# A fixed start order, a route in three steps, and a gate that ScalarE sums, in an attention and two-MoE kernel

## The chip, the cores and the metric

The kernel runs on one core of one Trainium2 chip. The metric is the device time of one execution in microseconds, as the median of several runs. TensorE is PE, VectorE DVE, ScalarE ACT, GpSimd POOL and SyncE SP.

## The reference

```python
# x: 8 batches, 8 heads, 576 tokens, 64 columns a head; 4608 tokens of 512 in all
kv = einsum('bhsd,bhde', q, einsum('bhsd,bhse->bhde', k, v))   # linear attention, no softmax
x = kv / sqrt(mean(kv*kv, -1) + 1e-6) * g_norm
# MoE1, dense: d_model 512, d_ff 1536
g = x @ w_gate;  x = (g * sigmoid(g) * (x @ w_val)) @ w_out
# MoE2: 8 experts, d_ff 1024; a token with x @ w_skip <= 0 is passed through
logits = xc @ w_gate2;  e = argmax(logits)
p = exp(logits - max(logits));  p /= sum(p) + 1e-9
y = p[e] * (relu(xc @ w1[e]) @ w2[e]);  out = xc + y
```

All is float32.

## The kernel before

The 4608 tokens go in 12 chunks of 384 (three rows of 128). A matmul in float32 is made of parts: each operand is split into a high and a low part (the ScalarE copy makes the high one, line 254 on POOL or VectorE the low one), and three products are summed.

**Attention.** Two heads are a pair, four pairs `pr` a chunk. `attn_load` loads k and v of a pair (`kv`, as 112 and 4 partitions, by `spread`) and its q (`qt`). `attn_unit` makes `kvp` (L211), copies it into `kvbd` (L213, L214), multiplies (`op`, L227), squares on ScalarE (`sq`, L233), reduces on VectorE (`ms`, L235 and L236), takes the power on POOL (`y`, L238) and scales (`xn`, L240). `make_xT` transposes that (`xtps`, L262) into `xT` (L265, L266). The units of chunk c+1 are worked between the steps of chunk c; those of chunk 0 stand at the program's start.

**MoE1.** A chunk takes 12 steps f. A step has 24 matmuls `gv` (L346), the silu (L352), a product on VectorE (`s`, L353), its split `hT` (L355, L254) and 9 matmuls `acc` (L367). The 18 weight tiles come in another number format and are converted during chunk 0: six VectorE instructions of about 0.7 us each tile (`split_bits`, L286, L287 and L290), with ScalarE (L284, L296) and POOL. They stay in the 18 buffers of pool `wp`; before that, four of these hold the q of chunk 0.

**Route.** The logits of chunk c−1 are worked on VectorE in chunk c, as 27 instructions `dump` (L400), 3 a step and 4 in the last chunk. Then `chunk_route` finds the expert and the place of each row (L432 to L452), with two small matmuls `rp` (L446, L447), and POOL scatters the rows to memory (`xs`, L454). The last chunk's own logits are made on TensorE: transposes `ltp` (L411) and matmuls `lps` (L416).

**MoE2.** Batches of up to 384 rows of one expert: batch 0 the first 256 rows of the fullest expert, ranked on the rows up to the chunk before the last, batch 1 the rest of it, then one batch for each other expert, and a rest. `load_xe` loads a batch's rows (L601, on `n // nt` partitions), `make_gate` makes the softmax weight (L584 to L591: maximum, difference, exponential, sum, reciprocal) and `make_xT2` transposes (`xtp`, L618; `xU`, L621 and L623). A step f has 12 matmuls `hp` (L633), the relu and split `h2T` (L641, L642), and matmuls `yacc` (L721) or `tacc` (L687). Expert weights `v` are split by ScalarE (L567) and by POOL or VectorE (L254). Work of batch 0 is interleaved with the end of the last chunk.

Each engine runs its instructions in order. That order isn't written by hand: the framework's scheduler takes the instructions in program order with a model of time and sets the order on each engine, within the dependencies and the orderings that `after(ins, to)` adds. SP issues nearly all loads, in order; a load whose completion lane or buffer is not free holds up those behind it.

Of the kernel before, what the change touches and what calls it, by code (L numbers as in the profile page):

```python
# [29 lines left out]
def attention_moe_moe_kernel(  # L30
# [97 lines left out]

    def attn_qt_load(c, pr):
        if c == 0:  # L130

# [4 lines left out]
        if c % 3 == 1:
            cut = S - T
            nc.gpsimd.memset(t[:, cut:cut + P], 0.0)
            nc.sync.dma_start(t[:, 0:cut], src[:, 0:cut])
            nc.sync.dma_start(t[:, cut + P:], src[:, cut:])  # L140
        else:
            nc.sync.dma_start(t[:, 0:T], src)
        qt[c, pr] = t

    def attn_load(c, pr):
        if c % 3 != 2:
            b = 2 * (c // 3) + c % 3
            t = p2.tile([P, 2, NR, P], F32, tag="kv", name="kv")
            for lo, hi in spread(PK):
                nc.sync.dma_start(t[lo:hi], kv_d[b, pr, lo:hi])  # L150
            kvt[c, pr] = t
        attn_qt_load(c, pr)

    attn_load(0, 0)


# [248 lines left out]
    def logits_pe(c, w9):  # L405
        lp = ps_acc.tile([P, R, P], F32, tag="acc", name="lps")
        for r in range(R):
            st = xrow[c, r]
            tp = ps_x.tile([P, NK, P], F32, tag="px", name="ltp")
            for kk in range(NK):  # L410
                nc.tensor.transpose(tp[:, kk, :], st[:, kk * P:(kk + 1) * P], ident)  # L411
# [3 lines left out]
            for kk in range(NK):  # L415
                nc.tensor.matmul(  # L416
# [7 lines left out]
    def chunk_route(c):  # L424
        lg = lgt.pop(c)
        wd = wdesc.rearrange("p (o e) -> p o e", o=1).to_broadcast([P, R, E])
        eb = (elast if c == NCH - 1 else ebase).rearrange("p (o e) -> p o e", o=1).to_broadcast([P, R, E])
# [19 lines left out]
        nc.tensor.matmul(rp, onesb, ca[:, 0:R, :], start=False, stop=True)  # L447
        nc.vector.tensor_tensor(oh, rp, eb, op=ALU.add)
# [128 lines left out]
    def make_gate(x, n, tag, q=P):  # L577
# [442 lines left out]
```

## Time and profile before

| | us |
|---|---|
| median of 3 runs | 1309.68 (1309.29 to 1310.69) |
| the profiled execution | 1305.69 |
| its span, first to last instruction | 1304.0 |
| PE busy | 1266.1 (97%) |
| POOL busy | 510.6 (39%) |
| DVE busy | 639.3 (49%) |
| ACT busy | 373.5 (29%) |

The mean granted clock of TensorE is 0.995 of full. A share of busy time is an average over the whole span; DVE at 49% is nine tenths busy in chunk 0 and a third in the last stage.

### The profile page before, as it was taken

To read this page: it belongs to the slowest core of one execution; us is meant where nothing else is said; L and a number is where in the kernel's file an instruction comes from. 1 tells how busy PE (TensorE), PEld (TensorE's weight loads), DVE (VectorE), ACT (ScalarE), POOL (GpSimd) and SP (SyncE) were. 2 spreads that over 40 slices of the span, in tenths; PEclk is the share of its full clock that TensorE was granted. 3 is DMA by queue.
4 is the path that set the end of the run, shared out by engine and by line. 5 is a ranking of instruction groups with operands and counts; after the bars stand their busy time and mean duration, and the time that the engine had idled before them with its cause. 6 is when DMAs were issued, how large, how long until landed. Compare 5 with 4: busy or idle time off the path is not lost.

```text
span 1304.0 us, 18975 instructions
## 1 busy us (share of the span) xinstructions
PE 1266.1 (97%) x7239; PEld 1180.2 (91%) x7239; DVE 639.3 (49%) x1487; ACT 373.5 (29%) x773; POOL 510.6 (39%) x545
## 2 busy tenths in 40 slices
PE   5998999999999999999999999999999989999997
PEld 5987999999999999999999999999988978899996
DVE  5896817237164371542815418146283243544662
ACT  3664112122121221211212112121122433344441
POOL 4674323233322332223323223223346443566662
PEclk9999999999999999999999999999999999999999
DMA  9663702021120111202102021110121343555631
GB/s 299 234 220 142 229 20 74 25 68 43 39 66 1 44 55 38 73 26 63 37 7 86 8 62 49 31 51 7 51 91 36 131 149 117 170 171 165 218 121 33
DMA packets 43205, 115.68 MB, mean 89 GB/s; under 512 B 8498, under 2 KB 16690, under 8 KB 40928
## 3 DMA queue, kind: packets, MB, share of 16 engines
q1 hardware_dynamic: 31888, 95.78, 22.7%
q0 software_dynamic: 6912, 9.82, 2.2%
q10 hardware_dynamic: 4304, 8.78, 2.1%
q8 instruction: 59, 0.97, 0.3%
q14 instruction: 42, 0.34, 0.1%
HBM read 88.70 MB, written 30.80 MB: 92 GB/s over the span
## 4 chain that ended last, share of the span: by engine, by line
PE 85%; DVE 5%; DMA 4%; POOL 3%; issue 2%; ACT 1%; SPq 0%; DVEq 0%; ACTq 0%; POOLq 0%
PE gv L346 42%; PE acc L367 21%; PE hp L633 7%; PE yacc L721 4%; PE tacc L687 3%; PE kvp L211 3%; PE op L227 2%; DVE dump L400 2%; PE xtps L262 1%; DMA kv<-in_kv_dram 1%; DMA xe<-xs_dram 1%; POOL v L254 1%; DMA raw<-in_w_dram 1%; DVE ex L585 1%; POOL w L254 1%
## 5 line engine op out<-in xcount | busy, mean ns | idle before, releaser
L346 PE MATMUL gv<-xT,w 128*128 128x384 f32 x3456 | 654.7, 339 | 3.8 <-ACT w L296 2.9
L346 PEld LDWEIGHTS gv<-xT,w 128*128 128x128 f32 x3456 | 602.1, 188 | 18.3 <-ACT w L296 4.2
L367 PE MATMUL acc<-w,hT 128*128 128x512 f32 x1296 | 333.3, 397 | 5.0 <-ACT hT L355 4.0
L254 POOL TENSOR_TENSOR hT<-s,hT 128x384 fp32r<-128x384 f32 x144 | 161.6, 1122 | 403.8 <-ACT hT L355 403.3
L367 PEld LDWEIGHTS acc<-w,hT 128*128 128x128 f32 x1296 | 239.3, 188 | 49.3 <-ACT hT L355 5.6
L400 DVE CUSTOM_DVE_ANT_0 dump<-st,w9b 128x512 bf16<-128x512 f32 x297 | 234.4, 789 | 7.0
L353 DVE TENSOR_TENSOR s<-gv,s 128x384 f32<-128x384 f32 x144 | 80.1, 556 | 253.0 <-PE gv L346 186.1
L254 POOL TENSOR_TENSOR v<-rawv,v 128x512 fp32r<-128x512 f32 x102 | 133.6, 1335 | 49.9 <-ACT v L567 49.7
L352 ACT ACTIVATE s<-gv 128x384 f32<-128x384 f32 x144 | 70.6, 490 | 260.4 <-PE gv L346 251.2
L355 ACT ACTIVATE hT<-s 128x384 fp32r<-128x384 f32 x144 | 75.5, 524 | 242.5 <-DVE s L353 241.1
L633 PE MATMUL hp<-xU,v 128*128 128x256 f32 (+7 forms) x768 | 125.8, 308 | 1.6 <-DVE xU L623 1.4
L633 PEld LDWEIGHTS hp<-xU,v 128*128 128x128 f32 x768 | 113.8, 189 | 4.7 <-DVE xU L623 1.7
L238 POOL TENSOR_TENSOR y<-ms,mhalf 128x6 f32<-128x6 f32 x48 | 68.2, 1422 | 109.7 <-DVE ms L236 107.8
L235 DVE TENSOR_REDUCE ms<-sq 128x6 f32<-128x384 f32 x48 | 26.4, 550 | 105.7 <-ACT sq L233 105.7
L567 ACT ACTIVATE v<-rawv 128x512 fp32r<-128x512 f32 x128 | 73.0, 623 | 1.9 <-DMA rawv<-in_v_dram 1.9
L721 PE MATMUL yacc<-v,h2T 128*128 128x512 f32 (+3 forms) x288 | 73.3, 397 | 0.0
L642 DVE SCALAR_TENSOR_TENSOR h2T<-hp,h2T 128x256 fp32r<-128x256 f32 (+7 forms) x64 | 30.5, 479 | 82.3 <-ACT h2T L641 81.1
L721 PEld LDWEIGHTS yacc<-v,h2T 128*128 128x128 f32 (+3 forms) x288 | 50.6, 181 | 11.2
L687 PE MATMUL tacc<-h2T,v 128*128 128x318 f32 (+3 forms) x384 | 58.1, 302 | 2.1 <-ACT h2T L641 2.1
L641 ACT ACTIVATE h2T<-hp 128x256 fp32r<-128x256 f32 (+7 forms) x64 | 27.2, 428 | 104.7 <-PE hp L633 92.1
L254 POOL TENSOR_TENSOR w<-raw,w 128x512 fp32r<-128x512 f32 x34 | 44.7, 1318 | 30.4 <-ACT w L296 29.5
L687 PEld LDWEIGHTS tacc<-h2T,v 128*128 128x128 f32 x384 | 53.8, 189 | 2.9 <-ACT h2T L641 2.8
(131 smaller groups left out, 875.8 us busy)
## 6 DMA issues: line engine op xcount, KB each, us to landing
rawv<-in_v_dram SPq DMA_DIRECT2D x64, 512.0 KB
kv<-in_kv_dram SPq DMA_DIRECT2D x32, 560.0 KB
raw<-in_w_dram SPq DMA_DIRECT2D x17, 1024.0 KB
out_dram<-st SPq DMA_DIRECT2D x36, 256.0 KB
xs_dram<-zrow ACTq DMA_DIRECT2D x8, 781.5 KB
qt<-in_qT_dram SPq DMA_DIRECT2D x32, 192.0 KB
qt<-in_qT_dram SPq DMA_DIRECT2D x32, 96.0 KB
w9b<-in_w_dram ACTq DMA_DIRECT2D x3, 768.0 KB
```

What stands on the lines that cost most here:

```text
L238: nc.gpsimd.tensor_tensor(y, ms, mhalf[:, 0:G], op=ALU.pow)
L254: return eng.tensor_tensor(lo, raw, hi.bitcast(F32), op=ALU.subtract)
L346: nc.tensor.matmul(pt, w1t[f][:, wi, i, kk, :], xT[c, kk][:, xi, :], start=(n == 0), stop=(n == 3 * NK - 1))
L352: step["silu"] = nc.scalar.activation(s, ps[0], AF.Silu)
L353: nc.vector.tensor_tensor(s, ps[1], s, op=ALU.mult)
L355: nc.scalar.activation(h[:, 0, :], s, AF.Copy)
L367: nc.tensor.matmul(acc[c, r], hT[c, f][:, hi, r * P:(r + 1) * P], w[:, wi, f % 2, :], start=(f == 0 and n == 0), stop=(f == NF - 1 and n = ...
L400: nc.vector.tensor_tensor_reduce(out=dump, in0=xrow[c, r][:, 0:DM], in1=w9b[m // 3][:, m % 3, :], op0=ALU.mult, op1=ALU.add, scale=1.0, sc ...
L567: after(nc.scalar.activation(w[:, 0, s], raw[:, s], AF.Copy), behind)
L633: nc.tensor.matmul(pt, w[:, wi, kk, cs], xT["m", b, kk][:, xi, :], start=(i == 0), stop=(i == 3 * NK - 1))
L687: nc.tensor.matmul(acc["m", b, d], w[:, wi, f % 2, d * P:(d + 1) * P], h[:, hi, :], start=(f == 0 and n == 0), stop=(f == NF2 - 1 and n == 2),
L721: ins = nc.tensor.matmul(acc["m", b, t][0:q], h[:, hi, t * q:(t + 1) * q], w[:, wi, f % 2, :], start=(f == 0 and n == 0), stop=(f == NF2 - ...
```

## The change

Five edits.

1. The k and v of a pair load in one DMA on 128 partitions (12 of them rows that aren't used). In chunk 0 each pair has its k, v and q in one buffer of pool `wp` (`kvq`), and the order of issue is written out: kv0, q0, kv1, q1, kv2, then the first weights, q2, kv3, q3. The units 2 and 3 stand behind the first weights' conversion in program order. Chunk 1's loads are ordered behind the conversion of the second weight tile, and that tile's conversion behind `ms` and `xn` of pair 3.
2. The route is in three parts: `chunk_route` to `rp`; a step later `route_rows` (place and scatter); another step later the ranking of experts, and for the last chunk the start of batch 0 and its load. Parts two and three are ordered behind the step's product L353.
3. `make_gate` negates the maximum on VectorE, and ScalarE takes the exponential of each column of rows with it as bias and sums in the same instruction. It is asked for at the batch's own f = 4, not at f = 2 of the batch before.
4. `load_xe` is one DMA on 128 partitions.
5. Batch 0's `hp` from f = 1 on and its `yacc` are ordered behind the last chunk's `ltp`, `lps` and `rp` on TensorE.

```diff
+    def attn_kv_load(c, pr, t, behind=None):
+            row = (b * NPR + pr) * PK
+            n = min(P, B * NPR * PK - row)
+            for lo, hi in spread(n):
+                after(nc.sync.dma_start(t[lo:hi], kv_rows[row + lo:row + hi]), behind)
...
+    def attn_load_first(pr):
+        t = wp.tile([P, 2 * NR * P + T], F32, tag="w", name="kvq")
+        attn_kv_load(0, pr, t[:, 0:2 * NR * P].rearrange("p (s r c) -> p s r c", s=2, r=NR))
+        return t[:, 2 * NR * P:]
...
+        step["rp"] = nc.tensor.matmul(rp, onesb, ca[:, 0:R, :], start=False, stop=True)
+        chosen[c] = rp, oh, m1, mk
+    def route_rows(c, behind=None):
+        after(nc.vector.tensor_tensor(oh, rp, eb, op=ALU.add), behind)
...
-        nc.vector.tensor_tensor(
-            ex[0:q], lg, m[0:q].rearrange("p (r o) -> p r o", o=1).to_broadcast([q, n, E]), op=ALU.subtract
-        )
-        nc.scalar.activation(ex[0:q], ex[0:q], AF.Exp)
-        nc.vector.tensor_reduce(m[0:q], ex[0:q], axis=AX.X, op=ALU.add)
-        nc.vector.tensor_scalar(m[0:q], m[0:q], 1e-9, None, op0=ALU.add)
-        nc.vector.reciprocal(gt[0:q], m[0:q])
+        nc.vector.tensor_scalar(m[0:q], m[0:q], -1.0, None, op0=ALU.mult)
+        for t in range(n):
+            nc.scalar.activation(
+                ex[0:q, t, :], lg[:, t, :], AF.Exp, bias=m[0:q, t:t + 1], accum_out=gt[0:q, t:t + 1]
+            )
+        nc.vector.tensor_scalar(gt[0:q], gt[0:q], 1e-9, None, op0=ALU.add)
+        nc.vector.reciprocal(gt[0:q], gt[0:q])
...
-        q = n // nt
-        for lo, hi in spread(q):
-            ins = nc.sync.dma_start(
-                fl(x[lo:hi]),
-                xs[bass.ds(xs_row[r] + (s0 + lo * nt), (hi - lo) * nt), :].rearrange("(p t) c -> p (t c)", t=nt),
-            )
+        return nc.sync.dma_start(
+            fl(x), xs[bass.ds(xs_row[r] + s0, P * nt), :].rearrange("(p t) c -> p (t c)", t=nt)
+        )
...
-    attn_load(0, 1)
+    attn_qt_load(0, 1, attn_load_first(1))
+    qt2 = attn_load_first(2)
     attn_unit(0, 0)
-    for pr in range(1, NPR):
-        if pr + 1 < NPR:
-            attn_load(0, pr + 1)
-        attn_unit(0, pr)
+    attn_unit(0, 1)
     load_w1(0, (step["ms", 0, 0], step["ms", 0, 1]))
+    attn_qt_load(0, 2, qt2)
+    attn_qt_load(0, 3, attn_load_first(3))
+    attn_unit(0, 2)
+    attn_unit(0, 3)
...
-    load_w1(1)
+    load_w1(1, (step["ms", 0, 3], step["xn", 0, 3]))
...
-                    attn_load(c + 1, f // 3)
+                    attn_load(c + 1, f // 3, conv_done.get(1) if c == 0 else None)
...
-                if f == -(-(E + 1) * R // lpf):
+                f0 = -(-(E + 1) * R // lpf)
+                if f == f0:
                     chunk_route(c - 1)
+                if f == f0 + 1:
+                    route_rows(c - 1, step["gv"])
+                if f == f0 + 2:
                     if c == NCH - 2:
-                        rank_experts(c - 1)
+                        rank_experts(c - 1, step["gv"])
                     if c == NCH - 1:
-                        early_base()
+                        early_base(step["gv"])
                         load_xe(0)
...
+    first_h = (None, step["ltp", 1], step["lps", R - 1], step["lps", R - 1], step["rp"])
+    first_y = (step["lps", R - 1], step["rp"])
...
-                load_gate(b + 1)
-            moe2_h(b, f)
+            if f == 4:
+                load_gate(b)
+
+            moe2_h(b, f, first_h[min(f, len(first_h) - 1)] if b == 0 else None)
```

How the order of instructions moves is shown at three places. A row is source line, operation, output from input, shape, and a count where it repeats; line numbers of the changed kernel are 9 higher around the start and 16 or 17 higher in MoE2. VectorE at the program's start, before, from the copy of pair 1's `kvp` to the first conversion (L286, L287, L290):

```order
L214 COPY kvbd_97<-kvp 64x64
L235 TENSOR_REDUCE ms<-sq 128x6
L236 TENSOR_SCALAR ms<-ms 128x6
L235 TENSOR_REDUCE ms<-sq 128x6
L286 TENSOR_SCALAR cv<-raw 128x512
L236 TENSOR_SCALAR ms<-ms 128x6
L287 SCALAR_TENSOR_TENSOR cv<-raw,cv 128x512
L240 TENSOR_TENSOR xn_190<-op,y 128x384
L290 SCALAR_TENSOR_TENSOR raw<-raw,cv 128x512
```

The same stretch of VectorE in the changed kernel:

```order
L223 COPY kvbd_95<-kvp 64x64
L244 TENSOR_REDUCE ms<-sq 128x6
L245 TENSOR_SCALAR ms<-ms 128x6
L223 COPY kvbd_99<-kvp 64x64
L244 TENSOR_REDUCE ms<-sq 128x6
L295 TENSOR_SCALAR cv<-raw 128x512
L249 TENSOR_TENSOR xn_188<-op,y 128x384
L245 TENSOR_SCALAR ms<-ms 128x6
L296 SCALAR_TENSOR_TENSOR cv<-raw,cv 128x512
L299 SCALAR_TENSOR_TENSOR raw<-raw,cv 128x512
```

The copy for pair 2 now stands ahead of pair 1's second `ms` and of the first conversion; before, it stood behind the first conversion. TensorE at the end of the last chunk, before, where the logits of the last chunk (`ltp`, `lps`) are made among batch 0's `hp` and `yacc`:

```order
L633 MATMUL hp<-xU_8842,v_2_8419 128x256 x2
L416 MATMUL lps<-w9k,lxt_8876 128x128 x2
L416 MATMUL lps<-w9k,lxt_8877 128x128 x2
L416 MATMUL lps<-w9k,lxt_8889 128x128 x2
L416 MATMUL lps<-w9k,lxt_8890 128x128 x2
L411 MATMUL ltp<-ident,st 128x128 x4
L721 MATMUL yacc_9060<-v_0_8264,h2T 128x512 x3
L721 MATMUL yacc_9064<-v_0_8264,h2T 128x512 x3
L721 MATMUL yacc_9060<-v_0_8264,h2T 128x512 x3
L721 MATMUL yacc_9064<-v_0_8264,h2T 128x512 x3
L633 MATMUL hp<-xU_8842,v_2_8419 128x256
L416 MATMUL lps<-w9k,lxt_8902 128x128 x2
```

The same place in the changed kernel:

```order
L648 MATMUL hp<-xU_8801,v_0_8178 128x256 x3
L648 MATMUL hp<-xU_8807,v_0_8178 128x256 x3
L425 MATMUL lps<-w9k,lxt_8841 128x128 x2
L425 MATMUL lps<-w9k,lxt_8842 128x128 x2
L420 MATMUL ltp<-ident,st 128x128 x4
L425 MATMUL lps<-w9k,lxt_8854 128x128 x2
L425 MATMUL lps<-w9k,lxt_8855 128x128 x2
L425 MATMUL lps<-w9k,lxt_8867 128x128 x2
L425 MATMUL lps<-w9k,lxt_8868 128x128 x2
L738 MATMUL yacc_9013<-v_0_8229,h2T 128x512 x3
L738 MATMUL yacc_9017<-v_0_8229,h2T 128x512 x3
```

The three rows' `lps` now follow one another ahead of the first `yacc`. VectorE at the end of batch 0, before, where `gm<-xe` is the first instruction that reads the rows of batch 1 (128x1) and of batch 2 (114x3), and `h2T<-hp` the low part of a step of batch 0:

```order
L850 TENSOR_SCALAR cnt<-nxt 128x8
L642 SCALAR_TENSOR_TENSOR h2T<-hp,h2T 128x256
L584 TENSOR_REDUCE gm<-xe 128x1
L585 TENSOR_TENSOR ex<-xe,gm 128x8
L623 TENSOR_TENSOR xU_9207<-xtp_9205,xU_9207 128x128
L623 TENSOR_TENSOR xU_9212<-xtp_9210,xU_9212 128x128
L589 TENSOR_REDUCE gm<-ex 128x1
L584 TENSOR_REDUCE gm<-xe 114x3
L590 TENSOR_SCALAR gm<-gm 128x1
L585 TENSOR_TENSOR ex<-xe,gm 114x24
```

The same place in the changed kernel:

```order
L875 TENSOR_SCALAR cnt<-nxt 128x8
L659 SCALAR_TENSOR_TENSOR h2T<-hp,h2T 128x256 x2
L602 TENSOR_REDUCE gm<-xe 128x1
L603 TENSOR_SCALAR gm<-gm 128x1
L608 TENSOR_SCALAR gt<-gt 128x1
L609 RECIPROCAL gt<-gt 128x1
L602 TENSOR_REDUCE gm<-xe 114x3
L659 SCALAR_TENSOR_TENSOR h2T<-hp,h2T 128x256
L603 TENSOR_SCALAR gm<-gm 114x3
L659 SCALAR_TENSOR_TENSOR h2T<-hp,h2T 128x256
L638 TENSOR_TENSOR xU_9160<-xtp_9158,xU_9160 128x128
L638 TENSOR_TENSOR xU_9165<-xtp_9163,xU_9165 128x128
```

Both first readers, of batch 1 and of batch 2, now stand ahead of the last two `h2T<-hp` of batch 0; on ScalarE the exponential of batch 1 stands ahead of the last two high parts in the same way.

## Rows read from the trace of the kernel before

**Rows 1.** TensorE's waits: line, releaser, us in total, times, longest.
```profile
PE xtps L262 <- DVE xn L240: 5.1, 1, 5.1
PE acc L367 <- ACT hT L355: 4.0, 4, 1.6
...
PE xtp L618 <- DMA xe<-xs_dram: 2.8, 1, 2.8
PE tacc L687 <- ACT h2T L641: 2.1, 3, 0.9
PE hp L633 <- DVE xU L623: 1.4, 1, 1.4
PE acc L367 <- POOL hT L254: 1.1, 3, 0.4
...
PE xtp L618 <- DVE xU L623: 0.4, 1, 0.4
```

**Rows 2.** Windows: length, busy PE, PEld, DVE, ACT, POOL (count), clock, DMA share, GB/s.
```profile
28.85:32.26 3.41, 3.37 (x13) 3.30 (x14) 3.36 (x6) 1.16 (x3) 1.61 (x2) 0.50 0.99 406
34.70:117.20 82.50, 77.05 (x423) 69.41 (x422) 72.33 (x118) 46.70 (x87) 56.04 (x49) 1.00 0.61 214
115.00:978.00 863.00, 862.09 (x4800) 807.39 (x4798) 405.01 (x1062) 188.62 (x387) 269.95 (x292) 1.00 0.17 53
1063.10:1066.50 3.40, 3.40 (x17) 3.40 (x18) 1.41 (x11) 1.06 (x5) 0.84 (x1) 0.50 0.92 333
```

**Rows 3.** Timeline of TensorE, the start: start, us, instruction [idle before <- releaser].
```profile
8.98 2.48 PE L211 MATMUL kvp<-kv 116*128 116x128 f32 x10 [0.36 <-DMA kv<-in_kv_dram]
...
16.21 2.47 PE L211 MATMUL kvp<-kv 116*128 116x128 f32 x10 [2.18 <-DMA kv<-in_kv_dram]
```

**Rows 4.** Timeline of VectorE, the start.
```profile
14.59 0.55 DVE L235 TENSOR_REDUCE ms<-sq 128x6 f32<-128x384 f32 x1 [0.52 <-ACT sq L233]
15.06 0.68 DVE L286 TENSOR_SCALAR cv<-raw 128x512 int32<-128x512 int32 x1
```

**Rows 5.** Timelines of VectorE and TensorE, the last chunk's first steps.
```profile
949.99 0.62 DVE L266 SCALAR_TENSOR_TENSOR xT<-xtps,g,xT 128x384 fp32r<-128x384 f32 x1 [1.64 <-ACT xT L265]
...
978.84 0.73 PE L367 MATMUL acc<-w,hT 128*128 128x512 f32 x2 [1.57 <-ACT hT L355]
978.87 1.54 DVE L400 CUSTOM_DVE_ANT_0 dump<-st,w9b 128x512 bf16<-128x512 f32 x1
...
987.75 1.42 PE L367 MATMUL acc<-w,hT 128*128 128x512 f32 x5 [0.41 <-POOL hT L254]
```

**Rows 6.** Timelines of four queues: last chunk's end, its route, the next rows.
```profile
1032.88 0.87 PE L367 MATMUL acc<-w,hT 128*128 128x512 f32 x3
1044.47 1.05 PE L416 MATMUL lps<-w9k,lxt 128*128 128x128 f32 x8
...
1052.28 0.17 DVE L452 TENSOR_SCALAR idx<-m 128x3 int32<-128x3 f32 x1
1053.38 0.43 DVE L642 SCALAR_TENSOR_TENSOR h2T<-hp,h2T 128x256 fp32r<-128x256 f32 x1
...
1058.55 1.70 SPq L601 DMA_DIRECT2D xe<-xs_dram  x3
1061.27 0.16 DVE L584 TENSOR_REDUCE gm<-xe 128x1 f32<-128x8 f32 x1 [4.64 <-DMA xe<-xs_dram]
1065.07 0.18 DVE L584 TENSOR_REDUCE gm<-xe 114x3 f32<-114x24 f32 x1 [1.26 <-DMA xe<-xs_dram]
```

**Rows 7.** Three lines' own views: count, ns min/median/max, first and last start.
```profile
L585 DVE TENSOR_TENSOR ex<-xe,gm x9: 174/184/4325, 1012.7 to 1245.2; 128x16 f32<-128x16 f32 x1, 128x8 f32<-128x8 f32 x1, 114x24 f32<-114x24 f32 x1, 124x24 f32<-124x24 f32 x1
L438 DVE TENSOR_SCALAR do<-lg x12: 158/171/1278, 155.2 to 1045.9; 128x3 f32<-128x3 f32 x12
L588 ACT ACTIVATE ex<-ex x9: 212/222/223, 1012.9 to 1249.4; 128x16 f32<-128x16 f32 x1, 128x8 f32<-128x8 f32 x1, 114x24 f32<-114x24 f32 x1, 124x24 f32<-124x24 f32 x1
```

**Rows 8.** Timeline of VectorE in batch 2, the gate of batch 3.
```profile
1081.99 0.18 DVE L584 TENSOR_REDUCE gm<-xe 124x3 f32<-124x24 f32 x1 [4.45 <-DMA xe<-xs_dram]
```

More of the change, by code (lines that the diff above doesn't have):

```diff
@@ L138, in attn_qt_load, with attn_load @@
             nc.gpsimd.memset(t[:, cut:cut + P], 0.0)
-            nc.sync.dma_start(t[:, 0:cut], src[:, 0:cut])
-            nc.sync.dma_start(t[:, cut + P:], src[:, cut:])
+            after(nc.sync.dma_start(t[:, 0:cut], src[:, 0:cut]), behind)
+            after(nc.sync.dma_start(t[:, cut + P:], src[:, cut:]), behind)
         else:
-            nc.sync.dma_start(t[:, 0:T], src)
+            after(nc.sync.dma_start(t[:, 0:T], src), behind)
         qt[c, pr] = t
-    def attn_load(c, pr):
+    def attn_load(c, pr, behind=None):
         if c % 3 != 2:
[L147 to L154, printed above, removed]
+            attn_kv_load(c, pr, p2.tile([P, 2, NR, P], F32, tag="kv", name="kv"), behind)
+        attn_qt_load(c, pr, p1.tile([P, T + P], F32, tag="qt", name="qt"), behind)
+    def attn_load_first(pr):
+        t = wp.tile([P, 2 * NR * P + T], F32, tag="w", name="kvq")
+        attn_kv_load(0, pr, t[:, 0:2 * NR * P].rearrange("p (s r c) -> p s r c", s=2, r=NR))
+        return t[:, 2 * NR * P:]
+    attn_qt_load(0, 0, attn_load_first(0))
     kvbd = {}
@@ L410, in logits_pe @@
             for kk in range(NK):
-                nc.tensor.transpose(tp[:, kk, :], st[:, kk * P:(kk + 1) * P], ident)
+                step["ltp", r] = nc.tensor.transpose(tp[:, kk, :], st[:, kk * P:(kk + 1) * P], ident)
             xt = [xtp.tile([P, 2, P], F32, tag=f"xn{2 * (r % 2) + i}", name=f"lxt{i}") for i in range(2)]
@@ L415, in logits_pe @@
             for kk in range(NK):
-                nc.tensor.matmul(
+                step["lps", r] = nc.tensor.matmul(
                     lp[:, r, :], xt[kk // 2][:, kk % 2, :], w9[:, kk, :], start=(kk == 0), stop=(kk == NK - 1)
@@ L480, in count, with by_rank @@
         return cp
-    def by_rank(src, name):
+    def by_rank(src, name, behind=None):
         t = xtp.tile([P, E, E], F32, tag="cmp", name="cmp")
-        nc.vector.tensor_tensor(t, sel, over(src, False), op=ALU.mult)
+        after(nc.vector.tensor_tensor(t, sel, over(src, False), op=ALU.mult), behind)
         o = p2.tile([P, E], F32, tag="rk" + name, name="rk" + name)
@@ L488, in by_rank, with rank_experts @@
         return o
-    def rank_experts(c):
+    def rank_experts(c, behind):
         key = p2.tile([P, E], F32, tag="key", name="key")
-        nc.vector.scalar_tensor_tensor(key, count(c), float(2 * E), wdesc, op0=ALU.mult, op1=ALU.add)
+        after(nc.vector.scalar_tensor_tensor(
+            key, count(c), float(2 * E), wdesc, op0=ALU.mult, op1=ALU.add
+        ), behind)
         t = xtp.tile([P, E, E], F32, tag="cmp", name="cmp")
@@ L512, in load_ranks, with early_base @@
             )
-    def early_base():
-        o = by_rank(count(NCH - 2), "o")
+    def early_base(behind):
+        o = by_rank(count(NCH - 2), "o", behind)
         nc.vector.tensor_scalar(adj, o[:, 0:1], -1.0, float(EARLY), op0=ALU.mult, op1=ALU.add)
@@ L623, in make_xT2, with moe2_h @@
         return nc.vector.tensor_tensor(xt[:, 1, :], tpf, xt[:, 0, :].bitcast(F32), op=ALU.subtract)
-    def moe2_h(b, f):
+    def moe2_h(b, f, behind=None):
         r, _, m, nt = BATCH[b]
@@ L632, in moe2_h @@
             for wi, xi in ((0, 0), (0, 1), (1, 0)):
-                nc.tensor.matmul(
+                ins = nc.tensor.matmul(
                     pt, w[:, wi, kk, cs], xT["m", b, kk][:, xi, :], start=(i == 0), stop=(i == 3 * NK - 1)
                 )
+                if i == 0:
+                    after(ins, behind)
                 i += 1
@@ L833, in attention_moe_moe_kernel @@
     chunk_route(NCH - 1)
+    route_rows(NCH - 1)
     load_xe(1)
```

25 lines of the change are left out of this document (12 added, 13 removed).

## The prediction

> **What bounds the kernel now.** I read TensorE's waits first [rows 1], then windows [rows 2], then the timelines of the engines where a wait ends. TensorE is busy 97% of the span, so the change can only win what TensorE stands still for, 1304.0 − 1266.1 = 37.9 us, plus what it loses at the half clock. From 115 to 978 us it is busy 862.09 of 863.00 us: ten of the twelve chunks hold nothing to win, whatever moves there, and their 405.01 us of VectorE and 188.62 of ScalarE show room for small additions. What can be won lies in three places. (1) The start and chunk 0. TensorE waits 5.1 us once for a scaled row (`xtps`), and runs 3.41 us at clock 0.50 (the 1.2 GHz level) behind that wait; later in chunk 0 it waits for converted weights. VectorE is busy 72.33 of the 82.50 us up to the last conversion, so it is the chain of conversions on VectorE, not TensorE, that sets when chunk 0 ends. (2) The last chunk: four waits for `hT` near 980 us [rows 1, 5]. (3) MoE2: one wait of 2.8 us for the rows of batch 1, with 3.40 us at half clock behind it, and single waits of about 1 us (`tacc`, `hp`).
>
> **Start and chunk 0.** Before, VectorE's first conversion starts at 15.06, right behind pair 1's second `ms`, which waited for the square [rows 4], which waits for `op` of pair 1; TensorE works that ahead of pair 2's `kvp`, which starts at 16.21 after a wait of 2.18 for its load [rows 3]. In the changed order pair 2's `kvp` stands ahead of that `op`, and pair 2's copy ahead of the `ms`. Its load is issued earlier: q2, q3 and the first weights no longer go ahead of it. I give it half of the 7.2 us that lay between pair 1's `kvp` (8.98) and pair 2's [rows 3], which makes 12.6, and take 13 instead of 16.2 (an estimate). Then `kvp` takes 2.47, `op` and the square some 2 us, so the conversion starts near 18.0 instead of 15.06: 3 us late, at the head of the chain that bounds chunk 0. Against that, pairs 2 and 3 are through attention earlier, and VectorE has 82.50 − 72.33 = 10.2 us of air further on, which a chain that runs later partly closes, where it waited for loads or for ScalarE that don't move. Were all of the delay kept, chunk 0 ends 3 us late; were the air used and the earlier loads worth something, it could end up to 3 us early. The row it is nearest to is the first conversion, late by 3, with two thirds of it closed by the air: I take +1.0 us (−3 to +3). The 5.1 us wait and the half clock after it may well change; that is worth nothing by itself, since VectorE is the bound until 117 us. The 12 unused rows make a load a tenth larger; with a DMA share of 0.17 in the middle they are hidden, and at the start they are in the 13 us.
>
> **Middle.** The route in three parts comes one step later and the gap between parts is a step; nobody waits for the rows until MoE2, so the cost is nothing. POOL's scatters and SP's load of batch 0 move by one step (862.09 us in some 137 steps gives 6.3 us). Batch 0's rows were there at 1012.7 [rows 7] and are used near the last sums (1032.88 [rows 6]), by an estimate some 6 us ahead of them: of about 14 us of cover, 8 are left. If that were gone, ScalarE and POOL would stand at their first reader with the weight splits behind it.
>
> **The last chunk, 978 to 988.** TensorE waits 1.57 first and 0.41 last, in four waits of together 2.95, since VectorE's product stands behind logits (`dump`), one of which takes 1.54 us [rows 5]. The number of `dump` per step is the same; moved by the change is the boundary of chunks 10 and 11, where VectorE idled (1.64 us at 949.99, and a like wait ahead of it) for `xT`, because TensorE's transposes stood ahead of the sums that the logits need. Now the nine last `acc` stand ahead of half of these transposes, so the logits can start 2 to 3 us earlier. I take half of the 2.95: −1.5 us (−2.9 to 0).
>
> **The end of the last chunk and batch 0.** Before: last `acc` 1032.88, last `lps` from 1044.47, places ready 1052.28, load of batch 1 issued 1058.55, read 1061.27, that of batch 2 read 1065.07 [rows 6]. So 11.6 us pass between the sums and the logits, in which `hp` and `yacc` of batch 0 went first. In the changed order only 18 `hp`, the 12 `ltp` and the 24 `lps` stand there. By the rows (8 `lps` 1.05, so 24 of them 3.2 and 12 `ltp` of the same shape 1.6; 3 `acc` of 512 columns 0.87, so 18 `hp` of 256 about 2.6) that is some 7 us, and the sums come some 2 us earlier because POOL makes the last `hT` behind fewer weight splits. So the logits end at 1036 to 1038 instead of 1045.5. From there to the places passed 6.8 us, of which `rp` stood 2 behind other matmuls; now some 5. From the places to batch 1's rows passed 9.0, and to batch 2's 12.8, which nothing shortens. That gives batch 1's rows at 1050 to 1052 and batch 2's at 1053.8 to 1055.8. The wait of 2.8 goes, with its echo of 0.4 [rows 1] and the half clock: 3.40 us at 0.50 is 1.7 us too many [rows 2]. A wait of 0.3 for `hT` from POOL goes too. Sum −5.2 us. What is late next: VectorE's first readers of both batches now stand ahead of the low parts of batch 0's last two steps, and ScalarE's exponential ahead of the high parts. Before, the low part of the last step but one came at 1053.38 [rows 6]. With batch 2's rows at 1055 it comes 1.8 us later, and I take TensorE to have 1 us of cover and a step's slip: +1.0 us (0 to 3).
>
> **The gate.** Each batch loses a difference and a sum on VectorE (0.18 us each by the median of L585) and gets a negation; ScalarE gets up to three exponentials of about 0.22 us for one [rows 7]. That is 0.44 us more ahead of an `h2T` in each of eight batches, and ScalarE is 29% busy: 0 on the path where ScalarE waits anyway, at most 0.44 where it doesn't. Where the gate is asked for hardly counts: in the order it still stands where it stood. So the wait at 1081.99, where VectorE stood 4.45 us for batch 3's rows ahead of `xU` [rows 8], stays; 1.4 us on TensorE, unchanged. The `tacc` waits (2.1 us in three) come from L585, whose median is 184 ns and which twice took over 4 us (4325 the longest) [rows 7], for as long as POOL's splits ran. L585 goes, but the negation L603 stands in its place. An instruction of its kind, L438, was held too: 171 ns median, 1278 the longest [rows 7]. The two long ones make 1.8 of the 2.1 (0.9 each). So I take 0 (−1.8 to +0.9, one such wait more).
> The Trainium skill (SBUF — State Buffer, "SBUF: two separate sides") says VectorE and GpSimd have one port pair between them, which one instruction holds for its whole length; on VectorE those with two SBUF inputs take part, and those with one only in a two-port mode. The long L585 rows agree. If the negation didn't run in that mode, the page would free it, and the sum would be 1.8 us lower; L438, which has one input, speaks against that.
>
> **Sum.** +1.0 − 1.5 − 5.2 + 1.0 + 0 = −4.7 us. The profiled execution takes 1305.69 us with a span of 1304.0; changed, about 1301.0. The median of the runs is 4.0 us above the profiled execution, and I put the difference on it: 1309.7 − 4.7 = **1305.0 us**.
>
> **Rivals.** *Given back at the start.* The chain of conversions keeps its 3 us, the last chunk wins nothing, the readers ahead of `h2T` cost 3 instead of 1: +3 + 0 − 5.2 + 3 = +0.8, 1310.5. For it: VectorE nine tenths busy in chunk 0. Against: 10.2 us of air. *Slower: the readers ahead of batch 0's last steps.* If the route of the last chunk gains 4 us rather than 10, batch 2's rows land at 1061; the low part of step 6 then waits from about 1054.4, where it is needed, 6.7 us, with 1.7 for the half clock again. That is 8.4 against the 4.9 that go (2.8, 0.4, 1.7): +3.5, and with +1.0, −1.5 and −0.3 it is +2.7, so 1312.4; with the 3 us of the start 1314.4; and with no gain in the route 1316. It decides from a landing of batch 2's rows at about 1060. For it: an engine's order is kept whatever lands late, and the route passes POOL and SP. Against: nothing but 18 `hp` now stands among the `lps` and `ltp`. *Better all over.* The start wins 3, the last chunk 2.9, the stall goes without a new one (5.2), the long holds vanish (1.8): −12.9, 1296.8. For it: all four have a mechanism; against: each has an order row against it, and the start above all. *The gate not in its own step* is in the sum already: its order hardly moves.
>
> **How the numbers follow.** Forecast 0.50, given back 0.20, slower 0.13, better all over 0.17. A measurement here can tell about 0.2%, 2.6 us: faster is below 1307.1, slower above 1312.3. Faster 0.50 + 0.17, less 0.03 for a forecast that falls 2 us short: 0.64. Same 0.20 + 0.03 less 0.01 for a given-back case that goes over: 0.22. Slower 0.14. The range goes from the best case, 1297, to just above the case given back, 1311; left out is the slower case and a little of each other.
>
> **What would show it.** In the changed profile: first conversion (L295) near 18 us, chunk 0's last conversion within 1 to 2 us of 117; `lps` over by 1038 and batch 1's rows read by 1052; no wait of TensorE on `xtp` there, and no half clock after it; TensorE's waits near 980 halved; the wait at batch 3's gate still there; one or two L603 of over 1 us. Wrong it would be made by a conversion chain that ends at 120 or later, or by a stall of TensorE on `yacc` at the end of batch 0.

## The result and the profile after

The changed kernel takes 1294.61 us (median of 4 runs, 1294.34 to 1295.65), the kernel before 1310.18 in the same comparison: a ratio of 0.988 (95% interval 0.9863 to 0.9897), 15.6 us less. The forecast was 1305.0 with a range down to 1297.0: the sign is right, and the gain is three times as large. The profiled execution takes 1294.39 us with a span of 1292.7, so by the two traces the gain is 11.3 us of span; the other 4.3 us lie between the first trace of the kernel before and its usual run (below).

The page and TensorE's waits of the changed kernel (line, releaser, us in total, times, longest), to be read beside [rows 1]:

```profile
span 1292.7 us, 18943 instructions
...
PE 1263.0 (98%) x7239; PEld 1176.4 (91%) x7239; DVE 639.6 (49%) x1478; ACT 380.4 (29%) x812; POOL 510.7 (40%) x545
```

```profile
PE kvp L220 <- DMA kvq<-in_kv_dram: 5.7, 2, 5.4
PE acc L376 <- ACT hT L364: 4.3, 5, 1.5
PE tacc L704 <- ACT h2T L658: 3.0, 3, 1.5
PE op L236 <- ACT raw L293: 2.4, 1, 2.4
PE op L236 <- DVE kvbd L223: 1.5, 1, 1.5
PE xtps L271 <- DVE xn L249: 1.1, 1, 1.1
```

Gone are the wait for the rows of batch 1 (2.8) and the one at batch 3's gate (1.4); `xtps` is down from 5.1 to 1.1; `tacc` is up from 2.1 to 3.0. Where the time goes, by the start of the same matmul in each trace, or its end where it says "done" (us from the span's start; chunk 1's first step is the `gv` after the first 288):

| | before | after | difference |
|---|---|---|---|
| first `gv` | 29.42 | 22.72 | −6.7 |
| chunk 1's first step | 121.54 | 118.02 | −3.5 |
| last chunk, step 5 | 981.66 | 978.03 | −3.6 |
| last chunk, step 6 | 989.48 | 984.78 | −4.7 |
| last `lps` done | 1045.52 | 1032.75 | −12.8 |
| batch 0, last `hp` | 1055.46 | 1049.65 | −5.8 |
| batch 3, first `hp` | 1109.96 | 1097.46 | −12.5 |
| span's end | 1303.98 | 1292.67 | −11.3 |

**The start.** TensorE, then VectorE, in the changed kernel (start, us, instruction, idle before):

```profile
11.63 1.28 PE L220 MATMUL kvp<-kvq 116*128 116x128 f32 x10
...
22.72 1.63 PE L355 MATMUL gv<-xT,w 128*128 128x384 f32 x4
```

```profile
14.14 0.55 DVE L244 TENSOR_REDUCE ms<-sq 128x6 f32<-128x384 f32 x1 [0.71 <-ACT sq L242]
14.61 0.68 DVE L295 TENSOR_SCALAR cv<-raw 128x512 int32<-128x512 int32 x1
```

Pair 2's `kvp` starts at 11.63 without a wait, against 16.21 [rows 3], and takes 1.28 us, not 2.47; the first conversion starts at 14.61, not late but 0.45 us early against [rows 4].

**The end of the last chunk, and batch 3.** VectorE in the changed kernel:

```profile
1032.79 0.18 DVE L428 COPY lg<-lps 128x27 f32<-128x27 f32 x1 [1.36 <-PE lps L425]
...
1046.82 0.16 DVE L602 TENSOR_REDUCE gm<-xe 128x1 f32<-128x8 f32 x1 [1.64 <-DMA xe<-xs_dram]
...
1050.48 0.18 DVE L602 TENSOR_REDUCE gm<-xe 114x3 f32<-114x24 f32 x1 [1.55 <-DMA xe<-xs_dram]
...
1069.14 0.18 DVE L602 TENSOR_REDUCE gm<-xe 124x3 f32<-124x24 f32 x1 [2.49 <-DMA xe<-xs_dram]
```

The rows of batches 1 and 2 are read 14.5 us earlier than in [rows 6]. VectorE waits for each of them, 1.5 to 2.5 us, and TensorE waits for none.

### The profile page after: what moved, and what is told of

Same layout as the page of the kernel before. It is cut to its first block, busy times and chain, and to the rows that moved or that the text cites. A ratio compares the mean times of both kernels' runs of the same rounds, so it can differ in the third digit from the quotient of the medians.

```text
span 1292.7 us, 18943 instructions
## 1 busy us (share of the span) xinstructions
PE 1263.0 (98%) x7239; PEld 1176.4 (91%) x7239; DVE 639.6 (49%) x1478; ACT 380.4 (29%) x812; POOL 510.7 (40%) x545
## 4 chain that ended last, share of the span: by engine, by line
PE 87%; DVE 5%; DMA 2%; issue 2%; POOL 2%; ACT 1%; SPq 0%; ACTq 0%; POOLq 0%; DVEq 0%
PE gv L355 43%; PE acc L376 22%; PE hp L648 7%; PE yacc L738 4%; PE tacc L704 3%; PE op L236 3%; PE kvp L220 3%; DMA raw<-in_w_dram 2%; DVE dump L409 1%; PE xtps L271 1%; DVE gm L603 1%; PE xtp L633 1%; DMA kvq<-in_kv_dram 0%; POOL w L263 0%; DMA rawv<-in_v_dram 0%
## 5 line engine op out<-in xcount | busy, mean ns | idle before, releaser
L585 ACT ACTIVATE v<-rawv 128x512 fp32r<-128x512 f32 x128 | 73.2, 623 | 1.5 <-PE gv L355 1.1
```

The costliest lines, as they stand in the source:

```text
L585: after(nc.scalar.activation(w[:, 0, s], raw[:, s], AF.Copy), behind)
```

## The experiments

Each was timed beside the kernel before, which took 1309.3 to 1309.8 us in the median each time; "the changed kernel" is its 1294.61 where no other time is given. The spread of four runs is 1 to 5 us, so differences under 2 us between medians are not told apart.

### The kernel before, once more

> The kernel before, unchanged, for a second trace. Its profiled execution was 4 us shorter than its median, that of the changed kernel 0.2 us. Theory: one stretch inside the span varies from run to run (loads at the start, or the half clock behind a stall); then the spans of these runs lie between 1304 and 1309 us as the times do, and this trace differs from the first in one place. Rival: the 4 us lie outside the span; then every span is near 1304 and the times near 1309.

1309.67 us (11 runs, 1307.82 to 1316.11). The spans lie from 1306.1 to 1314.4 with the times, so the 4 us are inside the span. The second trace is the longest of these runs, 10.4 us longer than the first. Its clock, and two of its half-clock stretches (columns as in [rows 2]):

```profile
core 0: 1314.4 us, clock 0.984
```

```profile
15.84:26.08 10.24, 8.79 (x38) 8.15 (x38) 7.43 (x15) 4.48 (x10) 3.73 (x3) 0.50 1.01 312
...
1067.14:1073.97 6.83, 6.50 (x28) 5.95 (x29) 4.39 (x15) 2.54 (x7) 2.92 (x4) 0.50 0.94 321
```

Ahead of the tail it has seven half-clock stretches (the first and the sixth are shown) of together 37.5 us; the first trace had two of 3.41. They begin in a stand of TensorE or within 1.5 us after one, the sixth at the end of the wait for batch 1's rows. So it isn't one place: the same stalls are followed by more half clock in one execution than in another. The other runs' mean clock is 0.989 to 0.994, the first trace's was 0.995; among the 13 runs of before in this comparison only one, 1305.89, was as short as it. The first trace was a lucky one. That the clock makes the whole of its 4 us is not shown: the run of 1305.89 has 0.992, one of 1309.48 has 0.994. Nor does the mean clock count everything: the view gives 1.00 for the first 20 us of the first trace, where ten `kvp` take 2.47 us [rows 3], as long as inside a half-clock stretch of the second (at 16.75), and 1.28 in the changed kernel at 11.63.

### The start taken back, and the start alone

```diff
-    attn_qt_load(0, 1, attn_load_first(1))
-    qt2 = attn_load_first(2)
+    attn_load(0, 1)
     attn_unit(0, 0)
...
-    load_w1(1, (step["ms", 0, 3], step["xn", 0, 3]))
+    load_w1(1)
```

This takes back the whole of edit 1: the loads of every chunk are in two pieces again and chunk 1's are ordered behind nothing. The second kernel is the one before with edit 1 alone.

> The changed kernel with the old start: loads of k and v in two pieces and in the old order, nothing ordered behind the first conversions. Theory: the start is worth what the traces show at chunk 1's first step, 3.5 us, so 1298 us. Rival A: it is also what makes the runs of before vary, then 1302 us. Rival B: the 3.5 us come from elsewhere in chunk 0, then 1294.6 us.

1301.1 us (1299.86 to 1302.26): 6.5 us more than the changed kernel. First `gv` at 30.86, chunk 1 at 124.59.

> The kernel before with the new start alone. Theory: 3.5 us less than the kernel before, 1306.7 us, with chunk 1's first step near 118 us. Rival A: 1302 us, if the start also takes away what varies. Rival B: 1310 us.

1301.26 us (1300.92 to 1304.56), 8 us less than the kernel before beside it (1309.3); first `gv` at 22.87, chunk 1 at 116.84. So the start is worth 6.5 to 8 us: rival A's number in both, and nearly twice what the first pair of traces shows. Rival A's reason is not shown with it: the four runs with the old start lie within 2.4 us, at a mean clock of 0.993 to 0.996.

### What bounds chunk 0

```diff
-        after(nc.vector.tensor_scalar(cv, low, 29, None, op0=ALU.logical_shift_right), behind)
-        nc.vector.scalar_tensor_tensor(
-            cv, high, -0x80000000, cv, op0=ALU.bitwise_and, op1=ALU.bitwise_or
-        )
+        after(nc.vector.tensor_scalar(cv, high, -0x80000000, None, op0=ALU.bitwise_and), behind)
```

> The kernel before with two VectorE instructions a half tile of weights instead of three: the lowest three mantissa bits of the weights are left out. That spares VectorE 36 times 0.7, 25 us, in chunk 0. Theory: in the kernel before TensorE bounds most of chunk 0, since it never idles from 32 to 83 us; then chunk 1's first step comes only some 5 us earlier (the waits of TensorE from 83 us on, 5.4), the first gv no earlier than 29 us. Rival (the prediction's reading): the chain of conversions on VectorE bounds chunk 0, then chunk 1's first step comes 10 to 25 us earlier.

> The changed kernel with the same two instructions instead of three (the lowest three bits left out). Theory: here TensorE starts 6.7 us earlier and waits for converted weights from 50 us on, so VectorE bounds chunk 0 in it; taken away, chunk 1's first step comes at 118 less the 5 to 7 us of waits, 111 to 113 us, some 7 us ahead of the same edit in the kernel before. Rival: the start's gain was in the conversions; then both kernels with the edit reach chunk 1 at the same time.

The lowest three bits of each weight are left out; three runs and two. Before: 1303.97 us, 5.4 less than the kernel before (1309.37), the theory's size, though VectorE is spared 25 us. After: 1285.28, 9.3 less than the changed kernel. In both traces nothing but TensorE is left as the bound: it waits at most 0.3 us between its first steps and chunk 1. So what the edit takes away is what the conversions cost in each. Chunk 1 comes at 115.31 and 106.46 (111 to 113 were expected for the second): the 8.9 us between them are what is left of the 9.4 us between the first `gv` (30.94 and 21.56). With the conversions out of the way, an earlier start of TensorE is kept nearly whole; by an estimate 1.7 of the 8.9 are half clock, of which the first has 6.83 us around its first `gv` and the second 3.41. The rows that show it stood in the trace of the kernel before, and the prediction does not use them. Windows 40 to 60 and 60 to 80 us, before and then after (columns as in [rows 2], TensorE the first busy time):

```profile
40.00:60.00 20.00, 20.00 (x112) 18.77 (x111) 18.22 (x31) 11.04 (x21) 12.61 (x12) 1.00 0.76 280
60.00:80.00 20.00, 20.00 (x122) 18.77 (x121) 17.30 (x29) 12.45 (x25) 14.99 (x14) 1.00 0.79 253
```

```profile
40.00:60.00 20.00, 19.67 (x116) 17.77 (x115) 18.47 (x32) 12.62 (x24) 12.77 (x13) 1.00 0.90 321
60.00:80.00 20.00, 18.57 (x101) 16.15 (x99) 18.08 (x30) 11.88 (x23) 13.26 (x12) 1.00 0.71 281
```

Before, TensorE has no air at all there while VectorE is nine tenths busy; after, VectorE is as busy and TensorE waits. The bound goes over from one to the other.

### Which part of the start

```diff
-    load_w1(1, (step["ms", 0, 3], step["xn", 0, 3]))
+    load_w1(1)
...
-                    attn_load(c + 1, f // 3, conv_done.get(1) if c == 0 else None)
+                    attn_load(c + 1, f // 3)
```

> The changed kernel without the two orderings in its start: chunk 1's loads not behind the second conversion, the second tile's conversion not behind pair 3's ms and xn. Theory: the gain of the start comes from the loads' order and the units' place, which give the first gv at 22.7 us; the orderings are worth under 1 us: 1294 to 1295.5 us. Rival: without them the second conversion delays pair 3's rows and the first gv, 1297 us or more.

1296.23 us (1294.56 to 1297.32), between theory and rival; its runs overlap those of the changed kernel. Its trace has chunk 1 at 116.81. The orderings are not shown to be worth anything.

```diff
-    qt2 = attn_load_first(2)
-    attn_unit(0, 0)
-    attn_unit(0, 1)
+    attn_qt_load(0, 2, attn_load_first(2))
+    attn_qt_load(0, 3, attn_load_first(3))
+    for pr in range(NPR):
+        attn_unit(0, pr)
     load_w1(0, (step["ms", 0, 0], step["ms", 0, 1]))
...
+    load_w1(1)
```

> The changed kernel with its loads in one piece and in their own buffers, all four pairs at once ahead of the first weights, but the units and the first conversions in the old program order and without the two orderings. Theory: the first gv comes at 21 to 24 us, since all pairs' rows are there early, and the conversion of the first tile then sets it: within 2 us of the changed kernel, 1294 to 1297 us. Rival: what counts is the first weights ahead of pair 3's loads; then the first conversion starts 3 us or more late and chunk 1 comes at 121 us: 1298 us.

1295.03 us (1294.05 to 1298.41), the changed kernel beside it 1294.97; first `gv` at 21.08. Neither the place of the units nor the first weights ahead of pair 3 is shown to be worth anything.

```diff
-            for lo, hi in spread(n):
+            for lo, hi in spread(PK):
```

> The changed kernel with each k and v load in two pieces as before (112 and 4 partitions). Theory: the second piece costs SP an issue of 0.4 us and a lane each, so that the loads of pairs 2 and 3 wait for a lane again: pair 2's rows land 1 to 2 us later, 1295 to 1297 us. Rival: the gain of the start is that of the single load as such; then 1299 us or more.

1300.81 us (1298.62 to 1302.5): with the loads in two pieces nearly the whole gain of the start is gone, 5.8 of the 6.5 us, all else being kept. The rival's time. SP's issue of pair 2's k and v in the changed kernel, then in this one, and TensorE in this one:

```profile
2.67 0.65 SPq L134 DMA_DIRECT2D kvq<-in_kv_dram  x1
```

```profile
3.31 3.21 SPq L134 DMA_DIRECT2D kvq<-in_kv_dram  x2
```

```profile
18.89 1.35 PE L220 MATMUL kvp<-kvq 116*128 116x128 f32 x10 [1.02 <-DMA kvq<-in_kv_dram]
```

The two issues for pair 2 take 3.21 us from the first's start to the second's end, since the second waits at SP until 6.28 (pair 0's `kvp` starts at 6.22); behind it stand the first weights, q2 and pair 3, whose `kvp` waits 1.02 and comes 2.2 us after the changed kernel's (16.73). Still, the first `gv` comes only 0.7 us later and chunk 1 1.9 (119.90). This trace has no half clock behind its first `gv`, where that of the changed kernel has 6.83 us:

```profile
21.67:28.50 6.83, 6.30 (x21) 5.69 (x22) 6.04 (x12) 4.43 (x9) 2.79 (x3) 0.50 0.92 377
```

If all 3.4 us of that are lost, by an estimate, the start makes 5.3 of the 5.8. But the two spans are 4.7 us apart (1297.4 and 1292.7), and 2.8 of these lie behind chunk 1's first step. So the 5.8 us of the single load are shown by the times, the way by which a second piece costs them only in part. What of it is the loads of chunk 0 and what those of chunk 1, which are in one piece too, was not tried apart.

### The changed kernel, once more

> The changed kernel, unchanged, for a second trace and more times beside the ones of this call. Theory: its time varies less than that of the kernel before (1305.9 to 1316.1), since fewer stalls of TensorE start a half-clock stretch: 1293 to 1297 us, mean clock 0.994 or more in each run, chunk 1's first step at 116 to 119 us. Rival: the four runs so far were narrow by chance, and it spreads over 8 us too.

1294.97 us (1291.74 to 1295.91), the theory's number. A narrower spread is not shown: it is 4.2 us, and the seven runs of the kernel before beside it lie within 2.0 (1309.02 to 1311.02). The mean clock is higher, 0.995 to 0.997 against 0.989 to 0.993. Chunk 1 comes at 115.40, and there is one half-clock stretch ahead of the tail, 6.83 us, in each of its two traces.

### The end of the last chunk

```diff
-    first_h = (None, step["ltp", 1], step["lps", R - 1], step["lps", R - 1], step["rp"])
-    first_y = (step["lps", R - 1], step["rp"])
+    first_h = (None,)
+    first_y = (None, None)
```

> The changed kernel without the ordering of batch 0 behind the last chunk's logits on TensorE. Theory: this ordering alone brings the logits and the route forward; without it the last logits end near 1041 in this time scale, TensorE stands some 2.8 us for batch 1's rows, then runs 3.4 us at half clock, and waits 1.4 us at batch 3's gate again: 1301 us. Rival: the earlier sums (POOL's order) and the gate's new form suffice, 1295 to 1297 us.

1298.1 us (1296.56 to 1299.64), 3.5 more, between the theory's 1301 and the rival's 1297. The last `lps` is done at 1039.30, and TensorE waits again, with 3.41 us of half clock behind it:

```profile
PE xtp L633 <- DMA xe<-xs_dram: 2.9, 1, 2.9
```

The wait at batch 3's gate does not come back, so that part of the expectation fell: its cause is another edit.

```diff
-                if f == f0 + 1:
-                    route_rows(c - 1, step["gv"])
-                if f == f0 + 2:
+                if f == f0:
+                    route_rows(c - 1)
```

> The changed kernel with the route in one part, as before, in the step where the logits end, and nothing of it ordered behind the step's product. Theory: the gain of 1.3 us near 980 us comes from the route's later instructions standing behind the product: without it 1296 us, with waits of 2.9 us there. Rival: it comes from the logits that start earlier at the chunk's boundary, then 1294.6 us and 1.9 us of waits.

1296.09 us (1294.87 to 1298.69), the theory's number, if within the spread. TensorE near 980 us with the route in one part (first two rows), and in the changed kernel (the third):

```profile
974.44 0.74 PE L376 MATMUL acc<-w,hT 128*128 128x512 f32 x2 [1.57 <-ACT hT L364]
...
983.35 1.91 PE L376 MATMUL acc<-w,hT 128*128 128x512 f32 x7 [0.42 <-POOL hT L263]
```

```profile
975.19 0.74 PE L376 MATMUL acc<-w,hT 128*128 128x512 f32 x2 [1.31 <-ACT hT L364]
```

The four waits are 2.94 us, the three that are left in the changed kernel 1.89. But with the route in one part the order at the boundary of chunks 10 and 11 goes back too (chunk 11's first step at 942.41 instead of 945.65), so theory and rival aren't told apart.

### The rows' load

```diff
-        return nc.sync.dma_start(
-            fl(x), xs[bass.ds(xs_row[r] + s0, P * nt), :].rearrange("(p t) c -> p (t c)", t=nt)
-        )
+        q = n // nt
+        for lo, hi in spread(q):
```

> The changed kernel with the rows of a batch loaded as before, on as many partitions as they fill, in two DMAs where that is no multiple of 16. Theory: nothing that can be measured, 1294.6 us. Rival: one issue less and one lane less let batch 3's rows be there in time, then the wait of 1.4 us at batch 3's gate comes back, 1296 us.

1298.23 us (1296.51 to 1301.51), 3.6 more: more than the rival. Batch 3's rows are issued at 1062.16, 0.75 us ahead of the changed kernel's (SP here, then in the changed kernel), and are read 1.56 later; TensorE waits for the `xU` behind that reader:

```profile
1062.16 0.89 SPq L620 DMA_DIRECT2D xe<-xs_dram  x2
```

```profile
1062.91 0.33 SPq L618 DMA_DIRECT2D xe<-xs_dram  x1
```

```profile
1070.70 0.18 DVE L602 TENSOR_REDUCE gm<-xe 124x3 f32<-124x24 f32 x1 [4.80 <-DMA xe<-xs_dram]
```

```profile
1071.55 0.74 PE L652 MATMUL hp<-xU,v 128*128 128x342 f32 x3 [1.68 <-DVE xU L642]
```

So the gate's wait that went (1.4) went with the single load. Another wait for `xU`, 1.08, stands at a later batch.

### The gate

```diff
-        nc.vector.tensor_scalar(m[0:q], m[0:q], -1.0, None, op0=ALU.mult)
+        nc.vector.tensor_tensor(ex[0:q], lg, m[0:q].rearrange("p (r o) -> p r o", o=1).to_broadcast([q, n, E]), op=ALU.subtract)
+        nc.scalar.activation(ex[0:q], ex[0:q], AF.Exp)
```

> The changed kernel with the old arithmetic of the gate (difference and sum on VectorE, one exponential for all columns). Theory: the gate's form is worth nothing or costs a little, since the negation is held by POOL's splits as the difference was and each exponential brings an instruction that reads the accumulator: 1293.5 to 1294.6 us, with TensorE's waits for h2T at 2.1 us instead of 3.0. Rival: it spares VectorE and ScalarE work on the path, 1296 us or more.

1293.36 us (1290.34 to 1295.28): the old arithmetic is not slower. `tacc` waits 0.90 and 0.96 us again. The new form wins nothing here.

```diff
-        nc.vector.tensor_scalar(m[0:q], m[0:q], -1.0, None, op0=ALU.mult)
+        nc.scalar.activation(m[0:q], m[0:q], AF.Copy, scale=-1.0)
```

> The changed kernel with the negation of the maximum on ScalarE instead of VectorE. Theory: the two waits of TensorE for h2T near 1210 and 1239 us (1.54 and 1.21) come from the negation being held on VectorE until POOL's splits end; on ScalarE it isn't held, the waits go, and it takes 1292 us. Rival: ScalarE's own three exponentials with their reads make the wait, and a fourth instruction adds to it: 1295 us.

1300.65 us (1297.38 to 1302.1), worse than either. The negation on VectorE in the changed kernel and POOL's row beside it, then the next small instruction on VectorE in this one, with POOL's row:

```profile
1204.26 4.34 DVE L603 TENSOR_SCALAR gm<-gm 90x3 f32<-90x3 f32 x1
```

```profile
1204.78 3.79 POOL L263 TENSOR_TENSOR v<-rawv,v 128x512 fp32r<-128x512 f32 x3
```

```profile
1206.05 6.90 DVE L608 TENSOR_SCALAR gt<-gt 90x3 f32<-90x3 f32 x1 [1.26 <-ACT ex L605]
```

```profile
1205.33 5.04 POOL L263 TENSOR_TENSOR v<-rawv,v 128x512 fp32r<-128x512 f32 x4
...
1210.44 2.47 POOL L263 TENSOR_TENSOR v<-rawv,v 128x512 fp32r<-128x512 f32 x2
```

The negation is no longer held; the addition of 1e-9 is, until POOL's row of splits ends, with `h2T` behind it, and TensorE waits 3.50 and 3.29 us, with 3.41 us of half clock behind each. The place of the hold moved, its cause stood.

```diff
-        nc.vector.tensor_reduce(m[0:q], lg, axis=AX.X, op=ALU.max)
-        nc.vector.tensor_scalar(m[0:q], m[0:q], -1.0, None, op0=ALU.mult)
+        nc.vector.tensor_reduce(m[0:q], lg, axis=AX.X, op=ALU.max, negate=True)
...
-        nc.vector.tensor_scalar(gt[0:q], gt[0:q], 1e-9, None, op0=ALU.add)
+        nc.scalar.activation(gt[0:q], gt[0:q], AF.Copy, bias=1e-9)
```

> The changed kernel with a gate that has no small elementwise instruction on VectorE: the reduction gives the negated maximum, ScalarE adds the 1e-9; a reduction and a reciprocal stay on VectorE. Theory: POOL's splits hold small elementwise instructions of VectorE (4.34 us the negation here, 6.90 the addition in the kernel with the negation on ScalarE) and no reductions; if the reciprocal isn't held either, the two waits of TensorE (1.54 and 1.21) go and it takes 1291.8 us. Rival: the reciprocal is held in its turn, then 1297 to 1301 us as with the negation on ScalarE.

1293.79 us (1293.54 to 1294.3), 2 us above the theory's number and well below the rival's. The reciprocal isn't held (176 ns the longest of nine), but VectorE's own split is, for 6.11 us, and TensorE still waits 0.81 and 1.01 us for `h2T`:

```profile
L608 DVE RECIPROCAL gt<-gt x9: 161/172/176, 1015.5 to 1241.3; 128x2 f32<-128x2 f32 x1, 128x1 f32<-128x1 f32 x1, 114x3 f32<-114x3 f32 x1, 124x3 f32<-124x3 f32 x1
```

```profile
1206.86 6.11 DVE L263 TENSOR_TENSOR v<-rawv,v 128x512 fp32r<-128x512 f32 x1 [0.63 <-ACT v L585]
```

```diff
-                sub_lo(raw[:, s], w[:, 0, s], w[:, 1, s], hold is not None and n_split[0] % VD == 0)
+                sub_lo(raw[:, s], w[:, 0, s], w[:, 1, s], False)
```

> The kernel with no small elementwise instruction in the gate, and in addition the low part of the expert weights made on POOL alone (before, every fourth half tile is made on VectorE). Theory: in that kernel VectorE's own split is held instead (6.11 us for a work of 0.7), with waits of 0.81 and 1.01 left on TensorE; without it these two go: 1291 to 1292 us. Rival: POOL then falls behind with the weights, and TensorE waits for them: 1296 us or more.

On top of the edit before, with all splits on POOL: 1291.91 us (1290.86 to 1293.43), a ratio to before of 0.9864 (0.9847 to 0.988), where the changed kernel beside it has 0.9889 (0.9873 to 0.9906). The two waits are gone:

```profile
PE tacc L703 <- ACT h2T L657: 0.2, 1, 0.2
```

This is the fastest that computes all of it, and the theory's number; its median is 3 us below the changed kernel's, with intervals that overlap.

## Why the prediction was wrong

Between the forecast of −4.7 us and the measured −15.6 lie, by an estimate from the rows above, 4.5 us at the start, 4.3 of the basis, 1.4 at batch 3's gate and 1.0 for readers that cost nothing; the gate (0.9) and 980 us (0.4) went the other way, and 1 us is not assigned.

**The bound of chunk 0: the step that failed.** The prediction took VectorE for the bound until 117 us, from its 72.33 of 82.50 us, and concluded that the 5.1 us wait and the half clock "may well change; that is worth nothing by itself". But the same row [rows 2] has TensorE at 77.05, more than VectorE; it had no wait from 32 to 81 us, and waited 5.4 us in all after that. An engine with nine tenths busy beside one with ten tenths is not the bound. So 6.7 us earlier at the first `gv` are worth what lies until the conversions catch up: 3.5 us in the two traces, 6.5 to 8 by the medians, not a cost of 1.0. The last conversion, before and after, which was to stay within 1 to 2 us of 117:

```profile
116.51 0.69 DVE L290 SCALAR_TENSOR_TENSOR rawh<-rawh,cv 128x512 int32<-128x512 int32 x1
```

```profile
112.98 0.69 DVE L299 SCALAR_TENSOR_TENSOR rawh<-rawh,cv 128x512 int32<-128x512 int32 x1
```

The chain started 0.45 us earlier and ended 3.5 earlier, so its own length did not set its end. The size of the delay fell as well: pair 2's `kvp` started at 11.63, taken as 13, and took 1.28 us, counted as 2.47; `op` of pair 1, though behind it, started at 12.75, and so the first conversion at 14.61, not 18.0.

**The basis.** The prediction took the 4.0 us between the profiled execution and the median for a constant. In the changed kernel they were 0.2 (1294.39 and 1294.61), so the medians gain 4.3 us more than the pair of traces; no term stood for that. The half clock behind stalls is the likely cause: the mean clock is 0.991 in the median over 46 further runs of the kernel before, 0.994 to 0.997 in the eight of the changed one, and 0.995 and 0.996 in the pair. Run by run the link is loose (above), so it is not shown.

**The end of the last chunk and batch 0.** Right in mechanism. The logits are done at 1032.75 (1036 to 1038 forecast), the rows read at 1046.82 (1050 to 1052) and 1050.48 (1053.8 to 1055.8); from step 6 of the last chunk to the last `lps` it is 8.1 us less, with 7.5 to 9.5 forecast. The wait, its echo and the half clock are gone, and the wait and the half clock come back when the ordering is taken back. The +1.0 for the readers ahead of `h2T` did not fall due: batch 2's rows are 4 us earlier than forecast, and VectorE's reader idles 1.55 us without holding TensorE. The slower rival stayed away for the same reason.

**980 us.** Forecast −1.5 by the earlier boundary; by the traces 2.95 became 1.89, −1.1. The size is right, the cause not settled.

**Batch 3's gate.** Forecast to stay, since its order stayed. It went with the single load: the prediction had costed that edit for the start alone and as bytes, not as a landing. The load in one piece was read 6.2 us after its issue, the one in two pieces 8.5 after the first and 8.0 after the second issue. Here and in the start, "one DMA on 128 partitions" was the edit that counted most, and the prediction gave it no term of its own.

**The gate.** Forecast 0 (−1.8 to +0.9); TensorE's waits grew by 0.9, the end of the range. The negation was held for 4.34 us as L585 had been for 4325 ns [rows 7], as the row of L438 foretold. What was not foreseen: each exponential takes 0.28 to 0.30 us and is followed by an instruction of 0.19 that reads the sum; from the first exponential's start to that of the `h2T` behind it pass 0.87 us (1208.64 to 1209.51) against 0.13 before (1220.99 to 1221.12), and the longest wait grew by 0.6. What the place changes, where the gate is asked for at its own step, was not tried apart.

## What to carry to other kernels

Take as bound in a stretch the engine whose waits there are zero, not one that looks busy, and look at short windows: 20.00 of 20.00 beside 18.22 decides. Compare a trace's time and mean clock with the other runs before adding terms onto it; a trace that is 4 us short can hide what stalls usually cost. And count a transfer by the time from issue to landing and by what its issue holds up, not by its bytes: a second piece of four partitions in the loads of k and v cost 5.8 us.

## What the runs showed of the hardware

While POOL runs splits back to back, an elementwise instruction of VectorE on operands in SBUF can wait for the end of the whole row of them: 4.34 us for 90x3 elements beside three, 6.90 for the same size beside six, 6.11 for 128x512. Not every one does. The addition of 128x1 ran its 0.15 us inside a row of two (POOL, then VectorE, in the changed kernel):

```profile
1047.00 2.54 POOL L263 TENSOR_TENSOR v<-rawv,v 128x512 fp32r<-128x512 f32 x2
```

```profile
1048.58 0.15 DVE L608 TENSOR_SCALAR gt<-gt 128x1 f32<-128x1 f32 x1 [1.42 <-ACT ex L605]
```

The conversions (0.68 to 0.70 us) and the low parts `h2T` (0.41 to 0.55), which read or write PSUM, were not held in the changed kernel, and the gate's reductions and reciprocals stayed at 158 to 179 ns. The Trainium skill (SBUF — State Buffer, "SBUF: two separate sides") has VectorE and GpSimd share one port pair that the loser waits for, and an instruction with one SBUF input takes part there only in a two-port mode; the negation has one and did take part, as its 4.34 us show. Taking the instruction away only passes the hold to the next of its kind; in the stretch near 1204 us TensorE was free of the wait when none was left. The half clock behind a stall lasted 3.41, 6.83 or 10.24 us in these traces, and how often it came differs between executions of one program: ahead of the tail 6.8 us in all in the first trace of the kernel before, 37.5 in the second.
